# Loading six weight tiles in pieces by partitions: an adaLN, linear-attention and GEGLU block on one core

## The chip, the cores and the metric

The kernel runs on one core of one Trainium2 chip, in one launch. The metric is device time in microseconds (us). The time before is 782.14 us, the median of three runs (781.69 to 782.68).

The core's engines are named as the profile names them. PE is the matmul engine and PEld its weight load. DVE, ACT and POOL are the vector, scalar and GpSimd engines. SP only issues DMAs here. A DMA is carried by up to sixteen DMA engines that work side by side; each of them marks its own share as complete, and the DMA has landed when all its marks are there.

## The reference

One token block (2048 rows of 1024) goes through a linear-attention part and a gated feed-forward part. Both are modulated by six vectors that are computed from `c`. All inputs and the output are bf16.

```python
mod = (silu(c) @ w_mod).reshape(1, 6, 1, 1024)
sa, ca, ga, sb, cb, gb = (mod[:, i] for i in range(6))
h = layernorm(x) * (1 + ca) + sa
q, k, v = split(h @ wqkv)                 # 32 heads of 32
pq, pk = phi(q), phi(k)                   # phi(t) = where(t > 0, t + 1, exp(t)) + 1e-6
kv = einsum('bhsd,bhse->bhde', pk, v);  z = pk.sum(s)
o = einsum('bhqd,bhde->bhqe', pq, kv) / (einsum('bhqd,bhd->bhq', pq, z) + 1e-6)
x = x + ga * (o @ wo)
h = layernorm(x) * (1 + cb) + sb
out = x + gb * ((gelu(h @ w_gate) * (h @ w_up)) @ w_down)
```

The change touches only the load of the part of `wqkv` that makes `k`.

## The kernel before

The program first writes a list of operations, each with the engine that runs it and the memory ranges it reads and writes. From the ranges it finds what each operation must wait for. `emit_stream` then emits each engine's operations in order, and before an operation it puts the semaphore waits that the operation needs.

The 2048 rows are sixteen chunks of 128. Chunks 0 to 3 form group 0 and chunks 4 to 7 group 1. The 1024 input channels are eight tiles `dc` of 128; the channels of a tile lie on the 128 partitions. `WK` holds the weights of `k` as eight such tiles, one for each `dc`, of 128 partitions by 1024 columns (2 KB in each partition, 256 KB in all).

The start of the kernel computes `k` for group 0. A chunk is normalized (DVE), transposed (PE) and copied to `h1T` (ACT). Each `dc` tile of it is then scaled and shifted by `1 + ca` and `sa` (DVE, line 724, `mods`). These factors come from `w_mod`. Its columns for `sa` and `ca` are loaded in four quarters `WMQ[q]`, each as two loads (`t` = 0 and 1, 512 KB each, in 512-byte pieces). Quarter `q` gives the factors of tiles `dc` = 2q and 2q + 1. The products with `silu(c)` run on PE (`mod_cols`, line 766), and DVE copies them out (`mod_copy`, line 775).

The PE order of this stretch is written out by hand. For the last quarters it is: `mod_cols` of quarter 2 with t = 0, one matmul, `mod_cols` of quarter 2 with t = 1, eleven matmuls of `k` (line 880, `kv_mm`), `mod_cols` of quarter 3 with t = 0, five matmuls (880 and 969, `k31`), `mod_cols` of quarter 3 with t = 1, three matmuls. After that, for each of the eight accumulators in turn, one matmul with tile 6 and one with tile 7 follow, and then the evacuation of the accumulators (`phi`, lines 869 to 872). Behind it run the 64 matmuls of `q` for group 0 (line 934, weights `WQ`). Then come the 64 matmuls of `k` for chunks 4 to 7 (line 880), whose rows arrive by the load `x_dma(4, 8)`. These later chunks are transposed by DMA (line 703).

All these loads are issued by SP, in one order. `Sched.dma` gives the DMAs of SP eight semaphores ("lanes") in rotation, and each DMA waits until the DMA eight places before it has landed. From the fourth load of `x` on, the order is: quarter 1 (t = 0, t = 1), tiles 2 and 3 of `WK`, quarter 2, tiles 4 and 5, quarter 3, tiles 6 and 7, then `WQ` in two loads of 512 KB (its first 512 columns, tiles 0 to 3 and 4 to 7), `x_dma(4, 8)` with 1 MB, and the other 512 columns of `WQ` with 1 MB. Lines 592, 598 and 603 are the issues of `x_dma`, `w_dma` and `wmq_dma`.

Of the kernel before, what the change touches and what calls it, by code (L numbers as in the profile page):

```python
# [10 lines left out]
P = 128  # L11
S = 2048
D = 1024
# [30 lines left out]
OFF_WK = OFF_YT  # L44
# [37 lines left out]


class Op:
    __slots__ = ("stream", "fn", "deps", "sem", "marked", "ticket", "is_dma", "idx", "note", "overwrite_ok", "ins", "num")

    def __init__(self, stream, fn, sem, is_dma, note=""):
        self.stream = stream
        self.fn = fn
        self.deps = []  # L90
        self.sem = sem
        self.marked = False
        self.ticket = None
        self.is_dma = is_dma
        self.idx = -1
        self.note = note


def rkey(op):
# [231 lines left out]
def bass_adaLN_cond__linear_attn_block__geglu_ffn__prompt_kernel(  # L331
# [18 lines left out]
    with ExitStack() as es:  # L350
# [6 lines left out]
        def at(name, shape, dty, off):  # L357
            return nc.alloc_sbuf_tensor_at(name, shape, dty, offset=ABASE + off, align_bytes=4)
# [19 lines left out]
        WK = at("wk", [P, NDC, D], bf16, OFF_WK)  # L378
# [75 lines left out]
        def r_xs(c0, c1):  # L454
            return [t_ for c_ in range(c0, c1) for t_ in r_x(c_)]
# [21 lines left out]
        def r_wv(g):  # L477
            return [(OFF_WK + g * 2048, OFF_WK + (g + 1) * 2048, "wv")]
# [25 lines left out]
        def r_w(off, name, dc, c0=0, c1=D):  # L504
            return [(off + (dc * D + c0) * 2, off + (dc * D + c1) * 2, name)]
# [14 lines left out]
        def r_wmq(i, t):  # L520
            return [(MSO[i] + (dc * 2 + t) * 512, MSO[i] + (dc * 2 + t + 1) * 512, f"wmq{i}") for dc in range(NDC)]
# [30 lines left out]
        sch = Sched()  # L552
        T, A, V, G, Q = PE_, ACT_, DVE_, POOL_, SP_
# [4 lines left out]
        wqkv_v = A_wqkv.rearrange("(c p) j -> p c j", p=P)  # L558
# [32 lines left out]
        def x_dma(c0, c1):  # L591
            return sch.dma(Q, lambda e: e.dma_start(XALL[:, c0:c1, :], x_v[:, c0:c1, :]), wr=r_xs(c0, c1), note=f"x{c0}")  # L592
# [4 lines left out]
        def w_dma(dst, off, name, kind, c0, c1, dc0=0, dc1=NDC):  # L597
            return sch.dma(Q, lambda e: e.dma_start(dst[:, dc0:dc1, c0:c1], wqkv_v[:, dc0:dc1, kind * D + c0:kind * D + c1]),  # L598
                           wr=[t_ for dc in range(dc0, dc1) for t_ in r_w(off, name, dc, c0, c1)], note=f"{name}.{dc0}.{c0}")

        def wmq_dma(q, ts=(0, 1)):
            for t in ts:
                sch.dma(Q, lambda e, t=t: e.dma_start(WMQ[q][:, :, t, :], wm_v[:, :, t * D + q * 256:t * D + (q + 1) * 256]),  # L603
                        wr=r_wmq(q, t), note=f"wmq{q}.{t}")
# [6 lines left out]
        x_dma(0, 1)  # L611
        x_dma(1, 2)
        wmq_dma(0, (1,))
        x_dma(2, 3)
        wmq_dma(0, (0,))
        w_dma(WK, OFF_WK, "wk", 1, 0, D, 0, 2)
        x_dma(3, 4)
        for q in range(1, 4):
            wmq_dma(q)
            for d0, d1 in ((2 * q, 2 * q + 1), (2 * q + 1, 2 * q + 2)):  # L620
                w_dma(WK, OFF_WK, "wk", 1, 0, D, d0, d1)
        w_dma(WQ, OFF_WQ, "wq", 0, 0, 512, 0, 4)
        w_dma(WQ, OFF_WQ, "wq", 0, 0, 512, 4, 8)
        x4_op = x_dma(4, 8)
# [517 lines left out]
        for c_ in range(10, NCH):  # L1142
            b = seq.index(("k", c_ // 2 * 2, 0)) - (9 if c_ % 2 else 12)
# [6 lines left out]
        for c_ in range(8, NCH, 2):  # L1150
            b = seq.index(("k", c_, 0)) - 3
# [10 lines left out]
        for g in range(NG):  # L1162
            task(nk + g // 2, lambda g=g: sch.dma(Q, lambda e: e.dma_start(WV[:, g, :, :], wqkv_v[:, :, 2 * D + g * P:2 * D + (g + 1) * P]),
                                                  wr=r_wv(g), note=f"wv{g}"))
# [688 lines left out]
        for n in range(12):  # L1853
            q, i = divmod(n, 4)
# [6 lines left out]
        for u in range(2 * NFP):  # L1861
# [5 lines left out]
            else:  # L1867
                a = ACTS.get(u, ((), ()))
# [83 lines left out]
        def emit_stream(stream):  # L1952
            ops = sch.streams[stream]

            def body(eng):
                waited = {}
                for o in ops:
                    need = {}
                    for d_ in o.deps:
                        assert d_.marked and d_.ticket is not None  # L1960
                        v = d_.ticket * (16 if d_.is_dma else 1)
                        if need.get(d_.sem, 0) < v:
                            need[d_.sem] = v
                    for sk, v in need.items():
                        if waited.get(sk, 0) >= v:
                            continue
                        eng.wait_ge(sems[sk], v)
                        waited[sk] = v
                    ins = o.fn(eng)
                    o.ins = ins  # L1970
                    if o.marked:
                        ins.then_inc(sems[o.sem], 16 if o.is_dma else 1)
                if stream == SP_:
                    finals = {}
                    for oo in out_ops:
                        finals[oo.sem] = sch.final_counts[oo.sem] * 16
                    last = max((oo for oo in out_ops if oo.stream == SP_), key=lambda oo: oo.idx)
                    for sk, v in sorted(finals.items(), key=lambda kv: kv[0] == last.sem):
                        eng.wait_ge(sems[sk], v)
            return body  # L1980
# [31 lines left out]
```

## Time and profile before

| | us |
|---|---|
| median of three runs | 782.14 |
| the profiled execution's own time | 781.62 |
| its span on the core | 779.8 |
| PE busy in the span | 773.0 |
| DVE busy | 647.4 |
| ACT busy | 377.3 |

From 26 us to the last matmuls at 775.5 us the view of PE's waits lists none: PE runs without a listed idle time. The first 26 us are the stretch in which PE waits.

The trace also has a time for each completion mark of a DMA. Every load below has sixteen, one for each DMA engine. The table gives the first, the fifteenth and the sixteenth of them, in us from the start of the span.

```
load                      first   15th    16th
WK tile 2                 14.62   14.87   14.89
WK tile 3                 15.33   15.59   15.61
quarter 2, t = 0          17.14   17.39   17.41
quarter 2, t = 1          18.82   19.09   20.64
WK tile 4                 19.49   19.77   21.32
WK tile 5                 20.21   20.49   22.03
quarter 3, t = 0          22.02   22.30   23.85
quarter 3, t = 1          23.79   24.07   25.53
WK tile 6                 24.46   24.74   26.19
WK tile 7                 25.14   25.42   26.84
WQ, 512 columns, 0 to 3   26.48   27.90   28.21
WQ, 512 columns, 4 to 7   27.93   29.45   29.81
x, chunks 4 to 7          31.26   32.65   32.93
WQ, other 512 columns     34.14   35.42   35.69
```

The load of `c` at the start has eight rows. Its semaphore shows one jump at 1.39 us and then eight marks from 2.00 to 2.09 us.

### The profile page before, as it was taken

The numbers are of one execution on the slowest core, as the hardware profiler recorded it, in microseconds if no ns is written. First come the engines' busy times: TensorE is split into PE (matmuls) and PEld (weight loads), VectorE is DVE, ScalarE is ACT, GpSimd is POOL, SyncE is SP. The second block draws the span as 40 slices with busy tenths as digits, with TensorE's granted clock in tenths as the row PEclk, the third lists the DMA queues.
The fourth block names the chain that finished last, engine by engine and source line by source line (L and its number), as shares of the span: only waits on it lengthen the run. The fifth ranks groups of instructions, "written<-read, shape, count | busy, mean of one in ns | idle before, by whom it ended". The sixth has DMA issues, their size and how long they took to land.

```text
span 779.8 us, 10832 instructions
## 1 busy us (share of the span) xinstructions
PE 773.0 (99%) x3883; PEld 496.9 (64%) x3883; DVE 647.4 (83%) x970; ACT 377.3 (48%) x635; POOL 49.2 (6%) x126
## 2 busy tenths in 40 slices
PE   8999999999999999999999999999999999999998
PEld 4444445666445667767676767667676567777766
DVE  6699988897898878787989888898989888667668
ACT  2497743242484487877755555555555211101111
POOL 2031300000331011100000000000000000000000
PEclk9999999999999999999999999999999999999999
DMA  9789749949996258967353865535357334443341
GB/s 290 250 169 251 157 94 221 258 125 203 209 271 182 82 147 204 237 169 215 104 140 110 261 203 168 149 96 162 98 146 223 111 123 142 137 148 98 132 143 54
DMA packets 196940, 130.22 MB, mean 167 GB/s; under 512 B 69516, under 2 KB 182420, under 8 KB 195864
## 3 DMA queue, kind: packets, MB, share of 16 engines
q1 hardware_dynamic: 196872, 129.55, 62.2%
q8 instruction: 30, 0.49, 0.3%
q14 instruction: 22, 0.18, 0.1%
q10 hardware_dynamic: 16, 0.00, 0.0%
HBM read 92.55 MB, written 23.35 MB: 149 GB/s over the span
## 4 chain that ended last, share of the span: by engine, by line
PE 96%; SPq 2%; DMA 1%; DVE 0%; issue 0%; DVEq 0%
PE ps_all L1472 45%; PE ps_all L1684 21%; PE ps_all L895 7%; PE ps_all L1292 7%; PE ps_all L934 7%; PE ps_all L880 6%; PE ps_all L1607 1%; SPq L598 1%; DMA wmq<-in_w_mod_dram 1%; SPq L603 1%; PE ps_all L913 0%; PE ps_all L1203 0%; PE ps_all L1246 0%; SPq L592 0%; PE ps_all L766 0%; PE ps_all L840 0%
## 5 line engine op out<-in xcount | busy, mean ns | idle before, releaser
L1472 PE MATMUL ps_all<-ss,tp 128*128 128x512 f32 x896 | 214.3, 396 | 0.0
L1472 PEld LDWEIGHTS ps_all<-ss,tp 128*128 128x128 f32 x896 | 168.2, 188 | 37.8 <-DVE ss L1427 0.3
L1472 PE MATMUL ps_all<-h2a,wt 128*128 128x512 bf16 x448 | 101.6, 380 | 0.0
L1684 PE MATMUL ps_all<-dt,sb 128*128 128x512 f32 x424 | 101.1, 394 | 0.0
L1495 ACT ACTIVATE ge<-ps_all 128x512 f32<-128x512 f32 x112 | 64.2, 597 | 73.8 <-DVE ps_all L1483 62.1
L1684 PEld LDWEIGHTS ps_all<-dt,sb 128*128 128x128 f32 x424 | 79.5, 188 | 17.9 <-DVE sb L1660 0.5
L1490 DVE TENSOR_TENSOR ps_all<-ps_all,es 128x512 f32<-128x512 f32 x54 | 37.6, 699 | 49.6 <-ACT es L1480 49.3
L1502 DVE TENSOR_TENSOR ys<-ge,ps_all 128x512 bf16<-128x512 f32 x112 | 74.5, 684 | 3.4 <-PE ps_all L1684 0.5
L1472 PEld LDWEIGHTS ps_all<-h2a,wt 128*128 128x128 bf16 x448 | 37.9, 97 | 57.3 <-ACT ps_all L1477 17.0
L1447 DVE TENSOR_TENSOR tp<-wt,tp 128x1024 fp32r<-128x1024 bf16 x56 | 68.3, 1220 | 0.0
L1447 DVE TENSOR_TENSOR tp<-wt 128x1024 fp32r<-128x1024 bf16 x56 | 68.2, 1218 | 0.0
L880 PE MATMUL ps_all<-wk,h1T 128*128 128x512 bf16 x248 | 56.8, 379 | 0.5 <-DVE h1T L724 0.5
L934 PE MATMUL ps_all<-h1T,wq 128*128 128x512 bf16 x256 | 56.7, 379 | 0.0
L1292 PE MATMUL ps_all<-w,pq 128*128 128x512 bf16 x256 | 56.4, 379 | 0.0
L1472 PE MATMUL ps_all<-ar,tp 128*128 128x512 f32 x224 | 55.5, 390 | 0.0
L869 ACT ACTIVATE eb<-ps_all 128x512 f32<-128x512 f32 x64 | 36.5, 595 | 38.2 <-PE ps_all L880 16.3
L1710 ACT ACTIVATE de<-ps_all 128x512 f32<-128x512 f32 x14 | 8.4, 599 | 90.2 <-PE ps_all L1684 90.2
L1684 PE MATMUL ps_all<-wd,ya 128*128 128x512 bf16 x212 | 47.7, 380 | 0.0
L1472 PEld LDWEIGHTS ps_all<-ar,tp 128*128 128x128 f32 x224 | 42.0, 188 | 8.8
L1477 ACT ACTIVATE ps_all<-ps_all 128x512 f32<-128x512 f32 x56 | 32.6, 583 | 30.7 <-PE ps_all L1472 30.7
L934 PEld LDWEIGHTS ps_all<-h1T,wq 128*128 128x128 bf16 x256 | 25.0, 98 | 30.0
L1292 PEld LDWEIGHTS ps_all<-w,pq 128*128 128x128 bf16 x256 | 24.7, 98 | 30.2 <-issue 1.1
(141 smaller groups left out, 992.2 us busy)
## 6 DMA issues: line engine op xcount, KB each, us to landing
wt<-in_B_w_gate_dram SPq DMA_DIRECT2D x28, 512.0 KB, 4.0
wt<-in_B_w_up_dram SPq DMA_DIRECT2D x28, 512.0 KB, 5.2
scr_y<-ys SPq DMA_DIRECT2D x28, 512.0 KB, 3.2
ya<-scr_y SPq DMA_DIRECT2D x14, 896.0 KB, 5.0
rb<-scr_rd SPq DMA_DIRECT2D x32, 256.0 KB, 6.4
wd<-in_B_w_down_dram SPq DMA_DIRECT2D x7, 1024.0 KB, 7.3
wmst<-in_w_mod_dram SPq DMA_DIRECT2D x6, 1024.0 KB, 5.8
wmq<-in_w_mod_dram SPq DMA_DIRECT2D x8, 512.0 KB, 6.9
```

The source lines that it names most:

```text
L869: sch.op(A, lambda e: e.activation(EB[i][:, :], PS(bank), ACTF.Exp), prd=pr(bank), wr=rng, note=f"{note}.exp")
L880: o = sch.op(T, lambda e, dc=dc: e.matmul(PS(bank), H1[sg][:, ci, dc, :], W_[:, dc, jg * 512:(jg + 1) * 512], start=(dc == 0), stop=(dc == ...
L895: o = sch.op(T, lambda e, c_=c_: e.matmul(PS(bank, 0, n), PK[c_][:, g * P:(g + 1) * P], xrow(c_, o_, o_ + n), start=(c_ == 0), stop=(c_ == ...
L934: o = sch.op(T, lambda e, dc=dc: e.matmul(PS(b), WQ[:, dc, qc * P:(qc + 1) * P], H1[sg][:, :, dc, :], start=(dc == 0), stop=(dc == NDC - 1 ...
L1292: last[half] = sch.op(T, lambda e, g=g, half=half: e.matmul(PS(b0 + half), PQ[sg][:, g, ci * P:(ci + 1) * P], W2[:, g, half * 512:(half + ...
L1447: sch.op(V, lambda e: e.tensor_tensor(TP[k][:], in0, in1 if k in (0, 2) else in1[:], ALU.subtract), rd=r0 + r1, wr=r_tp(k), deps=[x1_ops[7 ...
L1472: o = sch.op(T, lambda e, l_=l_, r_=r_, dc=dc: e.matmul(PS(b), l_, r_, start=fresh and dc == 0, stop=dc == ND2 - 1, skip_group_check=True) ...
L1477: sch.op(A, lambda e: e.activation(PS(BB + t), PS(BA + t), ACTF.Copy), prd=pr(BA + t), pwr=pr(BB + t), note="pcp")
L1490: sch.op(V, lambda e: e.tensor_tensor(PS(BC + t), PS(BC + t), ES[t][:, :], ALU.add), prd=pr(BC + t), rd=r_2k(OFF_ES[t], f"es{t}"), pwr=pr( ...
L1495: sch.op(A, lambda e: e.activation(GE[i][:, :], PS(b), ACTF.Gelu_apprx_tanh), prd=pr(b), wr=r_2k(OFF_GE[i], f"ge{i}"), note="gelu")
L1502: sch.op(V, lambda e: e.tensor_tensor(YS[s_][:, 2 * h:2 * h + 2, t, :], q(GE[i][:, :]), q(PS(b + 1)), ALU.mult), rd=r_2k(OFF_GE[i], f"ge{i ...
L1684: o = sch.op(T, lambda e, l_=l_, r_=r_, j=j, dst=dst: e.matmul(dst, l_[:, 0, :], r_, start=(k in (1, 5) or k == 7 and 0 < ca < 4 * CPG - 2 ...
```

## The change

Tiles 2 to 7 of `WK`, so far one load of 128 partitions each, are cut along the partitions: tiles 2 and 3 into 120 and 8, tile 4 into 126 and 2, tile 5 into 104 and 24, tile 6 into 88 and 40, tile 7 into 4, 8, 6 and 110. Six loads become fourteen. The bytes, their places and the order of the tiles among the other loads stay. The first piece carries the dependences of the whole tile; the other pieces hang on it in a list `more`, and whoever waits for the first waits for all of them, through one semaphore wait for each piece. Eight loads are added in all, as many as there are lanes, so every load behind tile 7 keeps its lane; but it now waits for another DMA, since the eight places before it hold smaller ones.

```diff
 class Op:
-    __slots__ = (..., "ins", "num")
+    __slots__ = (..., "ins", "num", "more")
...
         self.note = note
+        self.more = []
...
+        def parts(dst, src, cuts, **kw):
+            o = None
+            for a, b in zip((0,) + cuts, cuts + (P,)):
+                fn = lambda e, a=a, b=b: e.dma_start(dst[a:b], src[a:b])
+                if o is None:
+                    o = sch.dma(Q, fn, **kw)
+                    deps = [d for d in o.deps if not d.is_dma]
+                else:
+                    o.more.append(sch.dma(Q, fn, deps=deps, note=kw["note"]))
+            return o
+
+        def w_parts(c0, cuts):
+            parts(WK[:, c0:c0 + 1, :], wqkv_v[:, c0:c0 + 1, D:2 * D], cuts, wr=[t_ for t_ in r_w(OFF_WK, "wk", c0, 0, D)], note=f"wk.{c0}")
...
+        CUTS = {2: (120,), 3: (120,), 4: (126,), 5: (104,), 6: (88,), 7: (4, 12, 18)}
         for q in range(1, 4):
             wmq_dma(q)
-            for d0, d1 in ((2 * q, 2 * q + 1), (2 * q + 1, 2 * q + 2)):
-                w_dma(WK, OFF_WK, "wk", 1, 0, D, d0, d1)
+            for d0 in (2 * q, 2 * q + 1):
+                w_parts(d0, CUTS.get(d0, ()))
...
-                    for d_ in o.deps:
+                    for d_ in [x for d in o.deps for x in [d] + d.more]:
```

## The prediction

> **What bounds the kernel now.** I read the page first, then the chain that ended last in order of time, then the timeline where that chain leaves PE.
>
> ```profile
> span 779.8 us, 10832 instructions
> ...
> PE 96%; SPq 2%; DMA 1%; DVE 0%; issue 0%; DVEq 0%
> ```
>
> PE carries 96% of the chain. In order of time the chain shows where PE takes over:
>
> ```profile
> 15.53 0.43 SPq L598
> 15.96 0.04 issue
> 16.00 7.85 DMA wmq<-in_w_mod_dram
> 23.85 0.05 issue
> 23.90 0.55 PE ps_all L766 x16
> ...
> 25.58 0.55 PE ps_all L766 x16
> 26.13 3.81 PE ps_all L880 x17
> ```
>
> Up to 23.9 us loads set the pace; after 26 us it is PE without a break. So a microsecond won before 26 us reaches the end, unless a later wait, now covered, opens. The timeline of weight loads and matmuls, with idle time and its end in brackets, gives what can be won:
>
> ```profile
> 20.69 0.47 PEld L766 LDWEIGHTS ps_all<-siluT,wmq 128*128 128x128 bf16 x16 [1.12 <-DMA wmq<-in_w_mod_dram]
> ...
> 23.89 0.47 PEld L766 LDWEIGHTS ps_all<-siluT,wmq 128*128 128x128 bf16 x16 [0.64 <-DMA wmq<-in_w_mod_dram]
> ...
> 25.57 0.46 PEld L766 LDWEIGHTS ps_all<-siluT,wmq 128*128 128x128 bf16 x16 [0.52 <-DMA wmq<-in_w_mod_dram]
> ...
> 26.73 2.71 PEld L880 LDWEIGHTS ps_all<-wk,h1T 128*128 128x128 bf16 x14 [0.43 <-DVE h1T L724]
> ```
>
> Three waits end with the landing of a quarter of w_mod. Each of these landings is late by one mark: in the table of completion marks fifteen engines finish quarter 2, t = 1 by 19.09 and the sixteenth at 20.64, 1.55 us later, and this gap stays (1.46 at quarter 3, t = 1; 1.42 at tile 7). The DMA queues from 16 to 18 us show what came between:
>
> ```profile
> q1 hardware_dynamic: 1130, 0.57, 115.5%
> q8 instruction: 1, 0.02, 3.7%
> ```
>
> One 16 KB packet of another queue, an instruction fetch; the trace has it at 16.99 us for 1.19 us. One DMA engine stood for it, and since all engines are full it never catches up. Before the fetch the marks of a load come in a fixed order, spread over 0.27 us; afterwards the last place of that order is the empty one. So the late engine is one of the last to be served; its number the trace doesn't give.
>
> **The change part by part.** *Which engines carry a piece.* The rows: 128 partitions give sixteen marks, the eight rows of c give eight. I take from them that a piece goes over the largest count up to 16 that divides its partitions, and that the first engines are used. Then 120 goes over 15 engines with 8 packets each, 8 over 8, 126 over 14 (9 each), 2 over 2, 104 over 13 (8), 24 over 12 (2), 88 over 11 (8), 40 over 10 (4), 4, 8 and 6 over as many, 110 over 11 (10). The first engine gets 9, 9, 10, 10, 12 and 13 packets of tiles 2 to 7 instead of 8 each: 2 more by quarter 2, 6 more by quarter 3, 10 by the end of tile 6, 15 by that of tile 7. The last engine gets none of 48.
>
> *Price of a packet.* Tiles 6 and 7 are 0.68 us apart at the first mark (24.46, 25.14), with 8 packets of 2 KB on each engine: 0.085 us. The late engine needs 0.65 us for the same while others are elsewhere (26.19, 26.84), so a packet costs an engine its time whoever else runs, between 0.081 and 0.085. I take 0.085; the low bound, nothing at all, would hold if the engines shared one limit, and stays in the range.
>
> *Landings.* The late engine saves 16 packets by quarter 2: 16 x 0.085 = 1.36 us of the 1.55. Quarter 2, t = 1 then lands at 20.64 - 1.36 = 19.28. For quarter 3, t = 1 the first engine decides: 23.79 + 6 x 0.085 = 24.30, against 25.53. Tile 7: 25.14 + 15 x 0.085 = 26.42, against 26.84.
>
> *What PE makes of it.* The wait at 20.69 goes (PE is free at 19.6): -1.1 us. At 23.89 PE then waits for quarter 3, t = 0, which lands at 22.02 + 0.51 = 22.53: -1.3. At 25.57 it gets quarter 3, t = 1 at 24.30 instead of 25.53: -1.2. The matmuls with tile 6 would start at 25.5 and the first with tile 7 at 25.7; but tile 7 lands at 26.42. Here is the wait that takes the place: before, that matmul started at 26.97 (trace), 0.13 after tile 7's landing at 26.84, so tile 7 was already all but binding. Of 1.2 us, 26.84 - 26.42 = 0.42 are left.
>
> *Added waits.* PE waits for fourteen semaphores instead of six. One such wait took 51 ns in the trace; those of tiles 2 to 6 pass while PE's array is still behind. The three more of tile 7 cost nothing if the last piece is waited for, at most 0.15 us. Behind them stand the 16 matmuls with tiles 6 and 7. I take 0.05.
>
> *Added issues.* Eight more issues on SP, 0.43 to 0.48 us each by the short rows of its timeline: 3.8 us. They replace time in which SP is held:
>
> ```profile
> 7.28 3.80 SPq L598 DMA_DIRECT2D wk<-in_A_wqkv_dram  x2
> ...
> 12.87 3.09 SPq L598 DMA_DIRECT2D wk<-in_A_wqkv_dram  x2
> ...
> 19.12 3.33 SPq L598 DMA_DIRECT2D wk<-in_A_wqkv_dram  x2
> ```
>
> Two free issues take 0.9 us, so 2.9, 2.2 and 2.4 us are spare, against 1.0, 1.0 and 1.9 us added. By lanes the second WQ load now waits for quarter 3, t = 1 (24.30; issued at 22.97 before), and x for chunks 4 to 7 for tile 6's first piece (24.46 + 0.85 = 25.3; before 23.52). The first engine reaches x only after tile 7 and 1 MB of WQ, near 28.5, so this is covered for it; an engine with less work may run dry, which only gives its lead back.
>
> *What is late next.* x for chunks 4 to 7. It lands at 32.93, and ACT starts on it at once:
>
> ```profile
> 32.95 1.06 ACT L671 ACTIVATE xh<-xall 128x1024 bf16<-128x1024 bf16 x1
> ```
>
> From there ACT, the transposes and DVE lead to chunk 7's factors. Its last one ends at 55.79 + 0.31 = 56.10, and PE's matmul on it starts at 56.16, 0.29 after the one before instead of 0.22: no slack. So PE keeps a gain only as far as this chain moves too. Marks of x between 31.26 and 32.65 on engines that were not held, plus 1.27 (15 packets), are 32.5 to 33.9; engines with less work finish early and leave room. I take 32.7, 0.2 earlier. ACT's order also waits 0.23 us for PE at 47.92, just before chunk 7, which a faster PE gives back. So some 0.3 of 0.37 us survives.
>
> Sum: -0.42 + 0.05 + 0.07 = -0.3 us. The span goes from 779.8 to 779.5, the profiled execution from 781.62 to 781.3, and the median, 0.52 above that execution, from 782.14 to **781.8 us**.
>
> **The rivals.**
>
> *Pieces that block each other (slower).* In a 128-partition load the sixteen engines write without hindering each other (0.085). Cut otherwise, two engines may write at one time to partitions behind one entrance, and a packet takes twice as long. For it: nothing in the trace has another cut of this size. Against it: no 2 KB load here shows it. With 8 consecutive partitions on each engine (tiles 2, 3, 5 and 6) a tile costs 8 x 0.085 = 0.68 more: 1.36 by quarter 2, 2.04 by quarter 3, 2.7 by tile 7. Tile 7 lands at 26.42 + 2.7 = 29.1, 2.3 after 26.84: **784.4**. It decides from 0.42 / 4 = 0.1 us more for each of the four tiles. The Trainium skill, SBUF — State Buffer, section "Door 1: The DMA port swizzle", speaks for this: partitions p, p + 32 share one of sixteen ports, so engines that start 32 partitions apart meet. No run here shows it.
>
> *Free sharing out (better).* If the full engines lose nothing, tile 7 lands at 25.42, the k matmuls start 1.2 us earlier, x 1.5 earlier: 782.14 - 1.2 = **780.9**.
>
> *The late engine is not among those spared.* If pieces go to other engines than the first, and the late one gets the extra packets, tile 7 lands at 26.84 + 1.27 = 28.1: **783.4**. For it: the trace names no engine. Against it: the order of marks. The Trainium skill, DMA: Bandwidth & Descriptors, section "Why a DMA increments its semaphore by 16 and not by 1", states that SP's DMAs use the lowest-numbered engines; the trace can't show the number.
>
> *x late.* The forecast holds up to tile 7, but x lands at 33.9: 0.97 later, less 0.23: **782.9**.
>
> **How the numbers follow.** Forecast 0.36, blocking 0.26, free sharing 0.22, late engine 0.06, x late 0.10. About 0.2% (1.56 us) is what a measurement of this kernel can tell from no change. Of blocking I put 0.23 beyond it (the rest half-blocked and within), and 0.05 of late engine and x late, where both come together: slower 0.28. Free sharing is beyond it when PE also gets back the fetch's whole 1.55 us and some of the 0.43 that it waits for DVE at 26.73, about half of that case: faster 0.12. Same is the remaining 0.60. The range runs from 780.4 (free sharing with 0.5 us more) to 784.8 (blocking and 0.4 of x). The likeliest case alone has 781.2 to 782.4.
>
> **What would show it.** Right: the wait at 20.69 gone, no straggler among the marks of quarter 3, 15 and 8 marks for the pieces of tile 2, and PE standing before the first matmul with tile 7 until about 26.5. Wrong: tile 2's marks more than 0.9 us behind the load before it (blocking); a straggler as before (the late engine still carries pieces); chunk 7's factors done after 56.1 with PE waiting for them (x late). The forecast falls if tile 7 lands after 26.9, or before 26.0.

## The result and the profile after

The changed kernel takes 786.76 us (median of 4 runs, 786.24 to 789.0) against 782.29 for the kernel before (4 runs, 781.69 to 782.68): 1.0059 times as long, with a 95% interval of 1.0046 to 1.0073. It is slower by some 4.5 us; the forecast was 781.8 and its range ended at 784.8. The profiled execution of the changed kernel is the longest of its four, 789.0 us with a span of 786.8; the other spans are 784.0 to 784.9. The instructions stand in the same order on every engine, with line numbers about 16 higher (L766 is now L782, L880 is L896, L724 is L740), and the pieces are issued at L605.

From the page: the span and the shares of the chain that ended last.

```profile
span 786.8 us, 10845 instructions
...
PE 95%; SPq 3%; DMA 1%; issue 0%; DVE 0%; DVEq 0%
```

That chain in order of time (start, length, what):

```profile
26.08 5.67 DMA wk<-in_A_wqkv_dram
31.89 4.99 PE ps_all L896 x13
37.48 13.83 PE ps_all L950 x64
```

The place where PE takes over has moved from 26.13 us and quarter 3 to 31.89 us and the last piece of tile 7. Behind it PE runs to the end as before. So tile 7 is the last binding wait, as the forecast had it, but it lands at 31.75 us and not at 26.42. The timeline of weight loads (start, length, idle time and its end in brackets) shows the same loss growing from wait to wait:

```profile
22.66 0.47 PEld L782 LDWEIGHTS ps_all<-siluT,wmq 128*128 128x128 bf16 x16 [0.62 <-DMA wmq<-in_w_mod_dram]
...
26.52 0.46 PEld L782 LDWEIGHTS ps_all<-siluT,wmq 128*128 128x128 bf16 x16 [0.95 <-DMA wmq<-in_w_mod_dram]
...
28.91 0.48 PEld L782 LDWEIGHTS ps_all<-siluT,wmq 128*128 128x128 bf16 x16 [1.24 <-DMA wmq<-in_w_mod_dram]
...
31.86 0.14 PEld L896 LDWEIGHTS ps_all<-wk,h1T 128*128 128x128 bf16 x2 [1.24 <-DVE h1T L740]
```

The first three lines answer to 20.69, 23.89 and 25.57 of before and start 1.97, 2.63 and 3.34 us later. The fourth is the first weight load with tile 7. Its matmul started at 26.97 before and starts at 31.89 now, 4.92 us later. (The line at 26.73 of before begins with tile 6, whose weights now load at 30.51.) The last wait is put down to DVE, because the weights come from DVE; the timeline of matmuls names the load that was late.

```profile
31.89 4.99 PE L896 MATMUL ps_all<-wk,h1T 128*128 128x512 bf16 x13 [0.68 <-DMA wk<-in_A_wqkv_dram]
```

The completion marks tell the rest: of each load the first, the last but one and the last mark in us, for the kernel before, the changed kernel, and the changed kernel once more (the first experiment). A piece has as many marks as engines carry it, after one jump where they are fewer than sixteen.

```
load                marks  before               after                again
quarter 1, t = 1     16    13.94 14.20 14.23    14.11 16.57 16.82    13.89 15.64 15.75
tile 2, 120 rows     15    14.62 14.87 14.89    15.18 17.61 17.64    14.89 16.65 16.78
tile 2, 8 rows        8      (whole tile)       15.46 15.75 15.76    15.12 16.89 17.02
quarter 2, t = 0     16    17.14 17.39 17.41    18.02 20.03 20.15    17.18 19.38 19.43
quarter 2, t = 1     16    18.82 19.09 20.64    19.68 22.58 22.61    18.98 21.70 22.99
tile 5, 104 rows     13    20.21 20.49 22.03    22.09 24.62 24.64    21.69 23.65 24.90
tile 5, 24 rows      12      (whole tile)       22.41 24.87 24.91    21.90 23.93 25.12
quarter 3, t = 1     16    23.79 24.07 25.53    26.08 28.81 28.87    25.78 27.62 28.74
tile 6, 88 rows      11    24.46 24.74 26.19    27.36 29.91 29.93    26.87 28.12 29.77
tile 6, 40 rows      10      (whole tile)       27.79 30.28 30.41    27.16 28.75 30.27
tile 7, 8 rows        8      (whole tile)       28.00 28.79 30.65    27.64 29.23 29.32
tile 7, 110 rows     11    25.14 25.42 26.84    29.16 31.48 31.75    29.06 30.45 31.12
x, chunks 4 to 7     16    31.26 32.65 32.93    35.43 37.44 37.46    35.26 37.30 37.38
```

The pieces go over the engines that the forecast counted: 15 and 8 marks, 13 and 12, 11 and 10. But by the first marks, the engine that is furthest ahead needs 15.05 and 15.17 us from quarter 1, t = 1 to the end of tile 7, against 11.21 before: 3.9 us more. Of the eleven engines that reach the end of tile 7, the eleventh has 5 more packets than before and the first 15; at 0.085 us these are 0.4 to 1.3 us. The rest is that each packet takes longer. The DMA records have the time of every packet; those of 2 KB while the cut tiles load, in ns:

```
2 KB packets                  first quartile  median  third quartile  nine in ten below
before, 14 to 26 us                 85          88          93             109
changed, 14 to 31 us               100         118         139             155
changed, again                      95         116         136              -
before, 14 to 16 us                  -          87           -               -
changed, 14 to 16 us                 -         129           -               -
```

The stretch from 14 to 16 us, before and after, shows it too: the DMA engines are about as busy and move a third less (the last two columns are the DMA share and GB/s, the one ahead of them the granted clock).

```profile
14.00:16.00 2.00, 1.76 (x29) 1.22 (x28) 1.35 (x4) 0.55 (x1) 0.00 (x0) 1.00 1.11 343
```

```profile
14.00:16.00 2.00, 1.84 (x22) 0.78 (x20) 1.64 (x6) 0.48 (x1) 0.55 (x1) 1.00 1.05 238
```

One more thing is seen in the stretches of 2 us. The columns are busy us and counts by engine, then the granted clock, the DMA share and GB/s:

```profile
core 0: us, PE busy (x) PEld busy (x) DVE busy (x) ACT busy (x) POOL busy (x), PEclk, DMA share, GB/s
...
28.00:30.00 2.00, 1.25 (x19) 0.69 (x19) 0.45 (x3) 0.00 (x0) 0.00 (x0) 0.80 1.03 262
30.00:32.00 2.00, 1.32 (x4) 0.24 (x3) 0.88 (x4) 0.00 (x0) 0.00 (x0) 0.50 1.00 291
32.00:34.00 2.00, 2.00 (x6) 0.64 (x5) 0.83 (x2) 1.20 (x2) 0.00 (x0) 0.50 0.72 229
34.00:36.00 2.00, 2.00 (x6) 0.73 (x5) 1.78 (x5) 1.27 (x3) 0.00 (x0) 0.50 1.03 330
36.00:38.00 2.00, 2.00 (x18) 0.99 (x17) 2.00 (x5) 1.97 (x4) 0.00 (x0) 0.99 1.02 360
```

From some 29 to 36 us the granted clock is 0.50, and the matmuls behind tile 7 come every 0.43 us instead of every 0.22. Ten of them come before the clock is back, which is 2.1 us. With 4.91 us from tile 7's landing (31.75 against 26.84) this makes 7.0 us, all that the span grew by (786.8 - 779.8). It is why this execution is the longest of its four.

### The profile page after: what moved, and what is told of

The parts are those of the page before. It is cut to its first block, busy times and chain, and to the rows that moved or that the text cites. A ratio compares the mean times of both kernels' runs of the same rounds, so it can differ in the third digit from the quotient of the medians.

```text
span 786.8 us, 10845 instructions
## 1 busy us (share of the span) xinstructions
PE 777.2 (99%) x3883; PEld 498.2 (63%) x3883; DVE 647.5 (82%) x970; ACT 377.2 (48%) x635; POOL 48.1 (6%) x126
## 4 chain that ended last, share of the span: by engine, by line
PE 95%; SPq 3%; DMA 1%; issue 0%; DVE 0%; DVEq 0%
PE ps_all L1488 45%; PE ps_all L1700 21%; PE ps_all L911 7%; PE ps_all L1308 7%; PE ps_all L950 7%; PE ps_all L896 6%; SPq L605 2%; PE ps_all L1623 1%; SPq L618 1%; DMA wk<-in_A_wqkv_dram 1%; PE ps_all L929 0%; SPq L599 0%; PE ps_all L1219 0%; PE ps_all L1262 0%; SPq L593 0%
## 5 line engine op out<-in xcount | busy, mean ns | idle before, releaser
L896 PE MATMUL ps_all<-wk,h1T 128*128 128x512 bf16 x248 | 59.8, 393 | 1.1 <-DMA wk<-in_A_wqkv_dram 0.9
L896 PEld LDWEIGHTS ps_all<-wk,h1T 128*128 128x128 bf16 x248 | 24.2, 100 | 32.1 <-DVE h1T L740 4.0
```

The lines of the kernel that those rows point to most:

```text
L896: o = sch.op(T, lambda e, dc=dc: e.matmul(PS(bank), H1[sg][:, ci, dc, :], W_[:, dc, jg * 512:(jg + 1) * 512], start=(dc == 0), stop=(dc == ...
```

## The experiments

Diffs are against the changed kernel. The kernel before ran on the same chips: 781.9 us in the first four experiments (21 runs), 782.04 in the next four (19 runs), 782.67 (one run) in the last three.

**The changed kernel again.** Nothing is edited.

> The changed kernel once more, for a second profile: in the first one a DMA engine was already 1.8 us behind by the load of quarter 0 (last mark 7.93 us against 6.10 before), ahead of the first piece. If that lag belongs to the change, it is there again and the time is near 789 us; if not, the marks up to tile 2 are those of before, the time is 786 to 787 us, and tile 7 lands at 29 to 30 us. Whatever the theory: 786.2 to 787.

It took 787.1 us (4 runs, 785.06 to 789.2), ratio 1.0059 with an interval of 1.0037 to 1.0082. The last column of marks above is from its profile: span 784.5, 4.7 more than before, of which 31.12 - 26.84 = 4.28 is tile 7. In the pieces of tile 5 the last mark stands 1.2 us behind the last but one, in the 88 and 40 rows of tile 6 1.6 and 1.5 us, in the 8 rows of tile 7 only 0.1. The late engine still carries pieces, and here it is among the first ten engines but not among the first eight. In the first profile three engines lag from before the cut tiles on; none of them is among the first eight, since tile 2's 8 rows end at 15.76. After the instruction fetch (17.71 us in that execution) a fourth is late, and one mark of tile 7's 8 rows stands 1.86 us behind the others (28.79, 30.65). There the engine that became late is among the first eight. (The early lag is taken up with the kernel before.)

**Pieces by columns.** Fourteen pieces again, with the same waits and issues, but each over all 128 partitions:

```diff
-            for a, b in zip((0,) + cuts, cuts + (P,)):
-                fn = lambda e, a=a, b=b: e.dma_start(dst[a:b], src[a:b])
+            for a, b in zip((0,) + cuts, cuts + (D,)):
+                fn = lambda e, a=a, b=b: e.dma_start(dst[:, :, a:b], src[:, :, a:b])
...
-        CUTS = {2: (120,), 3: (120,), 4: (126,), 5: (104,), 6: (88,), 7: (4, 12, 18)}
+        CUTS = {2: (512,), 3: (512,), 4: (512,), 5: (512,), 6: (512,), 7: (256, 512, 768)}
```

> The same number of loads, waits and lanes, but each piece takes all 128 partitions and a part of the columns (512 and 512; tile 7 four times 256), so all sixteen engines carry the same and the partitions of one engine are those of before. Theory of blocking (two engines write to the same part of the partitions at one time): nothing is left of the loss but the price of the short packets, 782.2 to 782.9. Theory of uneven load (the first engines carry 15 packets more): the same, 782.2 to 782.9. Theory of issues (eight more loads hold SP, its lanes and PE's semaphore waits): the whole loss stays, 786 to 787.

782.97 us (10 runs, 782.24 to 784.55), ratio 1.0012 with an interval of 1.0003 to 1.0022. Here sixteen engines carry every piece. A half tile takes 0.36 to 0.42 us and the four pieces of tile 7 together 1.03 us, against 0.68 for a whole tile: shorter packets cost more for each byte. By the mean of their marks tiles 2 to 6 together took 0.35 us longer than before and tile 7 0.36. Not all of this is the packets: the first two pieces of tile 7 took 0.20 us each and the last two, with the same packets, 0.31 and 0.33, while the DMA share was only 0.74 and 0.66 from 25 to 27 us (0.96 and 0.90 before). There the engines ran dry behind SP's issues. The kernel lost 0.94 us by the ratio and 1.3 by the spans (781.1 against 779.8); with some 0.5 us for the shorter packets, 0.5 to 0.8 are left for waits and issues. Since this kernel has all the waits and issues of the changed one, 3.3 to 3.7 of that one's 4.6 us (0.59% of 782) come from cutting by partitions.

**Six tiles in halves by partitions.**

```diff
-        CUTS = {2: (120,), 3: (120,), 4: (126,), 5: (104,), 6: (88,), 7: (4, 12, 18)}
+        CUTS = {d0: (64,) for d0 in range(2, 8)}
```

> Every one of the six tiles cut into partitions 0 to 63 and 64 to 127. All sixteen engines carry 8 packets of a tile as before, but now each has 4 consecutive partitions of a half. Theory of blocking: packets of 2 KB take about 1.5 times as long (129 ns against 87 at the median in the first profile of the changed kernel), six tiles of 0.68 us become 1.0, tile 7 lands some 2 us later, 784 to 784.6. Theory of uneven load: no engine has more than before, 782.0 to 782.6. Theory of issues: six added loads of the eight, 785 to 786.

786.34 us (6 runs, 784.23 to 788.06), ratio 1.0046 with an interval of 1.003 to 1.0063. Each engine carries eight packets of each tile, as before, and the kernel is nearly as slow as the changed one. A half with four packets on each engine takes 0.47 to 0.57 us, so a packet takes about 0.13 us. The first engine, with no packet more than before, needs 14.09 us from quarter 1, t = 1 to the end of tile 7, against 11.21. I had expected the right direction from blocking and too small a size. The weight loads in the timeline wait for the same quarters as in the changed kernel:

```profile
22.36 0.47 PEld L782 LDWEIGHTS ps_all<-siluT,wmq 128*128 128x128 bf16 x16 [1.60 <-DMA wmq<-in_w_mod_dram]
...
26.01 0.47 PEld L782 LDWEIGHTS ps_all<-siluT,wmq 128*128 128x128 bf16 x16 [0.94 <-DMA wmq<-in_w_mod_dram]
...
28.85 0.51 PEld L782 LDWEIGHTS ps_all<-siluT,wmq 128*128 128x128 bf16 x16 [1.69 <-DMA wmq<-in_w_mod_dram]
```

An uneven load is thus not needed for the loss; cutting by rows is enough.

**Only two tiles cut, 126 and 2.** Here 14 engines carry nine packets each of tiles 2 and 3. If the late engine is one of the last two, it saves 16 packets.

```diff
-        CUTS = {2: (120,), 3: (120,), 4: (126,), 5: (104,), 6: (88,), 7: (4, 12, 18)}
+        CUTS = {2: (126,), 3: (126,)}
```

> Only tiles 2 and 3 are cut, into 126 and 2; tiles 4 to 7 whole. With 9 consecutive partitions on an engine, fourteen engines mostly start at different parts of the partitions. The last engines lose 16 packets ahead of the fetch (1.36 us of 1.55). Theory of blocking: packets little longer, two tiles cost the first engines 0.2 to 0.35 us each, tile 7 lands at 25.8 to 26.2 us instead of 26.84, 781.2 to 781.9. Theory of uneven load alone: 4 packets more on the first engine, 0.34 us, tile 7 at 25.8, 781.1 to 781.6. Theory of issues: two more loads, 783 to 783.5.

782.97 us (10 runs, 782.55 to 785.02), ratio 1.0013 with an interval of 1.0003 to 1.0022: slower, where both theories had it faster. The packets of 14 to 16 us have a median of 128 ns, so these two tiles do block, though nine rows on an engine were expected to collide little. And the straggler, the one mark far behind, stays: quarter 2, t = 1 has its last but one mark at 20.81 and its last at 22.14. The two engines that were spared lead from quarter 2, t = 0 (17.32 and 17.35, the third mark 18.23) to tile 4 (19.87 and 19.89, the third 20.61). So the late engine isn't one of them. Its profile, the longest of its runs, has the low clock too:

```profile
24.00:26.00 2.00, 2.00 (x7) 0.63 (x6) 0.00 (x0) 0.00 (x0) 0.00 (x0) 0.50 1.09 330
```

**Which engine is late, and which rows meet.** Rows are given one by one, with the piece to be measured first behind whole loads:

```diff
-            for a, b in zip((0,) + cuts, cuts + (P,)):
+            for a, b in cuts or ((0, P),):
...
-        CUTS = {2: (120,), 3: (120,), 4: (126,), 5: (104,), 6: (88,), 7: (4, 12, 18)}
+        MID = ((32, 96), (0, 32), (96, 128))
+        CUTS = {2: MID, 4: ((0, 64), (64, 128)), 6: MID, 7: ((0, 9), (9, 18), (18, 128))}
```

> Tiles 3 and 5 whole; the piece that comes first behind a quarter is read by its marks. Tiles 2 and 6 begin with partitions 32 to 95, tile 4 with 0 to 63: both have sixteen engines with 4 packets of 2 KB. In 32 to 95 engines e and e + 8 have partitions 32 apart from 64 on, in 0 to 63 they are 32 apart. Theory of blocking by shared entrances (partitions p and p + 32 within a half share one): from the last mark of the load before, 32 to 95 takes 4 x 0.085 = 0.34 us, 0 to 63 some 0.52 to 0.7 us. Theory that any load of less than 128 partitions is slow, or that every added load costs: both the same. Tile 7 begins with two pieces of 9 partitions (9 engines): a late engine that was in the pieces on 10 and 11 engines and in none on 8 or fewer shows here as the ninth mark about 1.2 us behind (it is the ninth engine) or not at all (the tenth). One time only, 783 to 785.5.

784.1 us (one run). The first piece of nine rows has eight marks from 26.38 to 27.42 and its ninth at 28.13; in the second it is 27.73 and 28.41. In the changed kernel's second profile a last mark by itself, 0.7 to 1.6 us behind, shows in the large pieces on 10 to 14 engines and in none on 4, 6 or 8. If it is one engine in both executions, it is the **ninth**. With tiles 6 and 7 alone cut (below) the straggler is again in the pieces on 11 and 10 engines and in none on 8, 6 or 4. But in the changed kernel's first profile it was the seventh or eighth (in the piece on 8 engines, not in that on 6), so it isn't the same engine in every execution. Every large piece of this change goes over the ninth: 8 + 8 + 9 + 8 packets of the larger pieces of tiles 2 to 5, 2 of tile 5's second piece, 8 + 4 of tile 6 and 10 of tile 7, 57 in all where it had 48. The seventh and eighth have 60. Rows 32 to 95 took 0.42 and 0.45 us by the mean of their marks, rows 0 to 63, with as many packets on as many engines, 0.52.

**Only tiles 6 and 7 cut.**

```diff
-        CUTS = {2: (120,), 3: (120,), 4: (126,), 5: (104,), 6: (88,), 7: (4, 12, 18)}
+        CUTS = {6: (88,), 7: (4, 12, 18)}
```

> Only tiles 6 and 7 cut as in the change, so the quarters of w_mod land as before. Blocking, with a late engine that carries 22 packets of the two tiles instead of 16: 6 x 0.085 + 22 x 0.042 = 1.4 us, tile 7 lands at 28.3 instead of 26.84, +1.4: 783.3 (782.7 to 784.0). Issues (four of the eight added loads): +2.3, 784.2. Uneven load without blocking: +0.5, 782.4.

**Only tiles 2 to 5 cut.**

```diff
-        CUTS = {2: (120,), 3: (120,), 4: (126,), 5: (104,), 6: (88,), 7: (4, 12, 18)}
+        CUTS = {2: (120,), 3: (120,), 4: (126,), 5: (104,)}
```

> Only tiles 2 to 5 cut as in the change. Blocking, with the late engine carrying 35 packets instead of 32: 3 x 0.085 + 35 x 0.042 = 1.7 us on quarter 3 and on tile 7, +1.7: 783.6 (783.0 to 784.6). Issues (four of eight): +2.3, 784.2. Uneven load without blocking: +0.3, 782.2. If this and the run with tiles 6 and 7 add up to less than 4.6 us, something that needs both is missing from the account.

The first took 784.0 us (10 runs, 783.02 to 786.93), ratio 1.003 with an interval of 1.0019 to 1.0041, the second 784.18 (10 runs, 783.09 to 786.39), 1.0026 with 1.0016 to 1.0036. Both lost 0.6 to 0.7 us more than blocking was expected to cost. Tile 7 lands at 28.91 and 30.19. The losses add up, 0.30% and 0.26% to the whole change's 0.59%: both groups of tiles pay. By their times alone these two kernels fit the theory of issues (784.2 for each) better than that of blocking; what speaks against issues is the kernel cut by columns, which has eight added issues and loses only 0.9 to 1.3 us.

**The kernel before again.** The edit takes the change out.

> The kernel before once more, for a second profile. In the first profile no packet between 2.7 and 14 us took over 140 ns; in all five of the cut kernels a dozen or more did, and quarter 1, t = 1 was complete at 15.2 to 16.8 us instead of 14.23, ahead of the first piece. If that belongs to the chip and not to the cuts, it is here too: quarter 1, t = 1 at 14.2 to 16 us and a time of 781.5 to 783.5. If it belongs to the cuts, it is 14.2 again.

781.31 us (one run), span 779.5. It settles one doubt. In the changed kernel's profiles some engines lag by 1.9 to 2.7 us at quarter 1, t = 1, before any cut tile (14.11 to 16.82 in the marks above, 13.89 to 15.75 in the second). Here they lag too, with marks from 13.45 to 15.34 where the first profile had 13.94 to 14.23; yet tile 7 lands at 26.68. Some packets of 2.7 to 9 us take over 140 ns in every profile but the first of the kernel before. The lag belongs to the execution and not to the change, and in this one execution whole tiles don't pay for it.

**Pieces of 16, 32, 64 and 96 rows.**

```diff
-        CUTS = {2: (120,), 3: (120,), 4: (126,), 5: (104,), 6: (88,), 7: (4, 12, 18)}
+        CUTS = {2: ((0, 16), (16, 32), (32, 128)), 4: ((0, 32), (32, 64), (64, 128)), 6: ((0, 64), (64, 128))}
```

(The loop over `cuts` is that of the two experiments with rows given one by one.)

> How the price of a packet goes with the rows of a load, read from the marks (mean over the sixteen engines, against the mean of the load before). Tile 2 is 0 to 15, 16 to 31 and the rest, tile 4 is 0 to 31, 32 to 63 and the rest, tile 6 two halves, tiles 3, 5 and 7 whole. Whole tiles took 0.65 to 0.72 us for 8 packets (0.085 each), halves 0.47 to 0.57 for 4 (0.13 each). Theory of shared entrances (rows in fours, p and p + 32 together): 16 rows reach 4 entrances, four engines on each: 0.2 to 0.3 us for the one packet; 32 rows and a half have two engines on each: 0.11 to 0.15 a packet. Theory that every load of fewer than 128 rows is slow alike: 0.12 to 0.13 a packet in all. Time 782.5 to 785.

784.86 us (one run). Sixteen engines carry each piece, with one packet for every 16 rows. By the mean of the marks:

```
rows of a piece     packets on an engine   us            us for a packet
16                          1              0.25, 0.24       0.25
32                          2              0.30, 0.28       0.15
64 (0 to 63)                4              0.57             0.14
96 (32 to 127)              6              0.45             0.08
128, whole (before)         8              0.68             0.085
```

From 32 rows down to 16 a packet takes longer, and 64 rows cost as much for each packet as 32, though the engines are sixteen each time. By itself this could also be a fixed cost of a piece, with the last piece of a tile catching up; the next two kernels have the same pieces and tell the two apart.

**Six tiles in three pieces, the same sizes, two sets of rows.**

```diff
-        CUTS = {2: (120,), 3: (120,), 4: (126,), 5: (104,), 6: (88,), 7: (4, 12, 18)}
+        CUTS = {d0: ((32, 96), (0, 32), (96, 128)) for d0 in range(2, 8)}
```

> All six tiles in rows 32 to 95, 0 to 31, 96 to 127. Beside it stands a run with 0 to 63, 64 to 95, 96 to 127: the same number of loads, rows, packets on each engine (4, 2, 2), waits and lanes. Only which rows are 64 together differs. Theory of shared entrances: the first piece of a tile here takes 0.34 to 0.45 us by the mean of its marks (sixteen engines on sixteen entrances), there 0.5 to 0.57; a tile 0.85 to 0.95 against 1.0 to 1.1; the time here is 0.3 to 0.9 us shorter. Theory that loads of fewer rows are slow alike, or that issues cost: no difference. 784 to 786.5.

```diff
-        CUTS = {2: (120,), 3: (120,), 4: (126,), 5: (104,), 6: (88,), 7: (4, 12, 18)}
+        CUTS = {d0: ((0, 64), (64, 96), (96, 128)) for d0 in range(2, 8)}
```

> All six tiles in rows 0 to 63, 64 to 95, 96 to 127: the partner of the run with 32 to 95 first. Shared entrances: first pieces 0.5 to 0.57 us, a tile 1.0 to 1.1, as with halves (786.3): 785 to 787.5. Otherwise as its partner.

784.94 and 786.56 us (one run each), with spans of 783.1 and 784.8. Both kernels have eighteen pieces of 64, 32 and 32 rows, and so the same packets, engines, waits and issues; only the rows differ. The first piece of a tile took 0.33 to 0.50 us in the one and 0.47 to 0.70 in the other. In each of the six tiles it is shorter with rows 32 to 95, by 0.8 us in all; the median packet of 14 to 31 us took 84 and 98 ns. The waits of PE from 14 to 38 us (us in total, times, longest), with rows 32 to 95 first and then with rows 0 to 63 first:

```profile
PE ps_all L782 <- DMA wmq<-in_w_mod_dram: 2.3, 3, 1.3
```

```profile
PE ps_all L782 <- DMA wmq<-in_w_mod_dram: 2.9, 4, 1.2
...
PE ps_all L896 <- DMA wk<-in_A_wqkv_dram: 0.4, 1, 0.4
```

The later landings reach the end: in the timelines of weight loads, the run of matmuls behind tile 7 starts at 29.56 and at 31.08.

```profile
29.56 2.50 PEld L896 LDWEIGHTS ps_all<-wk,h1T 128*128 128x128 bf16 x13 [0.70 <-DVE h1T L740]
```

```profile
31.08 2.50 PEld L896 LDWEIGHTS ps_all<-wk,h1T 128*128 128x128 bf16 x13 [0.63 <-DVE h1T L740]
```

These 1.52 us are nearly all of the 1.6 between the two times. But these are one execution each, and executions of one cut kernel lie further apart (784.23 to 788.06 in halves); at quarter 1, t = 1, ahead of the cut tiles, the last mark already stands at 15.62 in the one and 16.75 in the other. What the rows do is shown by the six pairs of pieces and the 0.42, 0.45 and 0.52 us above, and not by the 1.6 us. In both kernels the engines also run dry at times: from 14 to 16 us the DMA share is 0.77 and 0.84, against 1.11 before, so with eighteen pieces SP no longer stays ahead. In both the granted clock stays at 1.00 in this stretch. No run found a version that beats the kernel before.

## Why the prediction was wrong

- **What bounds the kernel** held. Loads set the pace, then PE runs to the end; what tile 7 loses arrives in the time one to one (spans less tile 7's landing: 753.0 before, 752.8 with the change taken out again, 753.2 by columns, 753.4 in the changed kernel again; 755.0 in its first profile, where 2.1 us go to the clock).
- **Which engines carry a piece** held: as many as the largest divisor up to sixteen, as the marks show. That smaller pieces use the first of the engines fits the late marks of the first profile (four in the pieces on 14 and 13 engines behind the fetch, three on 12, 11 and 10, one on 8, none on 6 and 4); no trace names an engine.
- **The price of a packet failed**, and this step cost most (halves, without any uneven load, lose 0.46% of the 0.59%). The forecast had "a packet costs an engine its time whoever else runs, between 0.081 and 0.085". Both numbers were read from whole tiles, in which all sixteen engines or one alone were at work, and neither case could show two engines in each other's way. In the changed kernel the median packet takes 0.118 us, in halves about 0.13. The same pieces on other rows, 0.33 to 0.50 against 0.47 to 0.70 us, show that the place of the rows is a cause by itself, and the halves that no uneven load is needed.
- The Trainium skill, SBUF — State Buffer, section "Door 1: The DMA port swizzle", states that partitions reach sixteen ports, and within each half of 64 p and p + 32 the same one. By it rows 32 to 95 reach sixteen ports and rows 0 to 63 eight; the trace agrees in the order (0.52 against 0.42 and 0.45 us) and not in a factor of two.
- **The late engine failed.** The forecast took it for "one of the last to be served" from the order of marks, and spared it 16 packets by quarter 2. The marks don't say that. They carry no engine's name, and the first fifteen marks of tiles 4 to 7 span 0.28 us, as much as all sixteen of tiles 2 and 3 (0.27 and 0.28, their first fifteen 0.25 and 0.26): the last place is still filled, and the engine that is missing stood further inside. It was the ninth in one reading and the seventh or eighth in another, and carries 9 to 12 packets more. At 0.085 us this puts it 0.8 to 1.0 us further back where it should have caught up, enough by itself to turn the sign; this price was worked out and not measured by itself.
- **The blocking rival** named the mechanism and was too small. It priced a packet too high (twice as long; the median went from 88 to 118 ns), but it left tiles 4 and 7 out, took the 512-byte quarters for unhindered, and had tile 7 at 29.1. It landed at 31.12 and 31.75. The quarters pay too: from t = 0 to t = 1 of quarter 2 the mean mark moves 1.78 us before, 1.91 and 1.98 in the changed kernel's profiles and 2.05 in halves, perhaps because an engine that lags with a piece writes beside others that have gone on to the quarter; no run shows the reason.
- **Added waits and issues** were priced low. The forecast had 0.05 us; the kernel cut by columns has all of them, and 0.5 to 0.8 us are left for them there. In the changed kernel SP stays ahead, if barely: its last piece of tile 7 is issued at 26.08 and the engines come to it from 28 us on.
- **Tile 7 as the new wait** held in its place; **x as what is late next** lost its meaning: x landed at 37.4 while PE, behind the same tile, was late by as much.
- **The clock** wasn't in the forecast at all. It costs up to 2.1 us in some executions and accounts for the slowest of the changed kernel (granted clock over the span 0.996 in the run of 789.0 us and 0.995 in that of 789.2), not for the median nor for the rest of the scatter (784.9 us of span at 1.00 in another run): the changed kernel again has 0.4 us over tile 7's delay, in halves 0.4, and the two kernels with other rows show their losses at full clock.

What stays open is how the 4.5 us divide between shared entrances, the 9 to 12 packets more on the late engine, and the issues; no run changed the uneven load alone. That neighbouring rows go to one engine was assumed in the theories of blocking; no trace names the rows of an engine. A cut that spares the late engine without sharing entrances wasn't tried.

## What to carry to other kernels

A load cut by partitions isn't made of the same packets as the whole: measure one such piece behind whole loads, by the mean of its completion marks, before its packets are priced. A duration read while all engines are spread evenly says nothing of the same engines when their rows lie close. To relieve one engine, first find its place in the order, by a load that uses few enough engines to leave it out, and see in a second execution whether it is the same one.

## What the runs showed of the hardware

- Behind an instruction fetch of one packet (1.19 us at 16.99 us), one DMA engine is late by 1.55 us, and with whole tiles it is so still at tile 7 (1.42).
- After idle times of 1.2 to 2.0 us in the timeline of weight loads PE's granted clock fell to 0.50, for 6.8 us in the changed kernel's first profile and for 3.4 us in its second, in halves, with two tiles cut and with tiles 6 and 7 cut; matmuls then came every 0.43 us. It didn't fall in the others, though the same timeline has idle times of 1.6 us with rows 32 to 95 first and 1.9 with tiles 2 to 5 cut; what decides it isn't settled. The Trainium skill, TensorE: Matmul & The Clock Gate, section "Part 1: The HAM clock gate", has a table of two states, full and half clock; the trace agrees in the two values.
- Some engines fall 1 to 2 us behind within the first 11 us in every profile but the first of the kernel before, without a cost to the kernel before: its time was 781.31 with that lag and 781.62 without it.
